# A new instruction order, and other engines for some copies, in a fused attention and gated feed-forward kernel

## The chip, the cores and the metric

The kernel runs on one NeuronCore of a Trainium2 chip. The metric is the device time of one execution in microseconds (us). Of the kernel before there are three timed runs.

## What is computed

Eight batches of eight heads, 576 tokens, head size 64. A small set of 32 packed queries p attends to k and v; then q attends to the packed result, which is key and value at once. The output, as 4608 tokens of 512, goes through a feed-forward network with d_ff = 2048.

```python
def sm_attn(qq, kk, vv):
    s = scale * np.matmul(qq, kk.transpose(0, 1, 3, 2))
    s = s - np.max(s, axis=-1, keepdims=True)
    a = np.exp(s)
    a = a / (np.sum(a, axis=-1, keepdims=True) + 1e-09)
    return np.matmul(a, vv)
p_packed = sm_attn(p, k, v)
out = sm_attn(q, p_packed, p_packed)
...
h = x @ w_in
g = h * (1.0 / (1.0 + np.exp(-1.702 * h)))
return (g @ w_out).astype(np.float32)
```

## The kernel before, in words

**Precision.** Everything is float32. An operand of the large matrix products is held in two parts, an upper part (a cast to fp32r) and a lower part (the rest), and a product is three matmuls: upper by upper, upper by lower, lower by upper. The upper part is made by a plain copy that may run on either of two engines (`move`: L111 is the copy on ScalarE, L113 the one on another engine, here VectorE). The lower part is a subtraction on VectorE.

**Attention.** For each batch b, `scores1_mm` (L275) makes the scores of the packed queries in two halves of 288 keys, `scores1_copy` takes them out of PSUM, `scores1_max` and `bias1` find the maximum, `exp1` (L331) exponentiates with a sum, the result is transposed through DRAM (or on TensorE for batches 0 and 1), `pack` (L415) multiplies by v. `pack_turn_mm` turns the packed result into PT. `m_mm` (L454) multiplies PT by one of four column blocks c of w_in; `m_upper` and `m_lower` (L478) split it. `scores2_mm` (L498) makes the second scores, `scores2_turn`, `max2`, `sub2`, `exp2` (L535), `sum2`, `norm2`, `turn2` the second softmax; `a_upper` and `a_lower` (L572) split it. So x itself is never made: h = a times m.

**Feed-forward.** d_ff is cut into two halves (phases). In a phase, for each batch, half of its tokens and each block u of 256 columns, `h_mm` (L604) makes h with two groups of six matmuls in a pair of PSUM banks. `g_main` (L621) takes 256 tokens, `g_over` (L626) the 32 that are left over, both on ScalarE with the gelu table; the left-over tokens of four batches are gathered into one more block, "over". `g_over` is the last reader of the pair, and so frees it. Then come `g_sum` (L664, block sums on VectorE), `g_upper` (the cast of 128x896), `g_lower` (L682), and `prod` (L745): seven block products in place of eight, into the four accumulator banks A to D. Their weights are prepared the same way: `begin_w` (L198, ScalarE) and `join_w` (L226, VectorE) put the two halves of a word of the raw load together, `wa_upper` and `wa_lower` (L236) split it, `w_diff` (L259) makes the block differences T, `wb_upper` and `wb_lower` split those. Batch 0 is done with plain products (`prod0`, L703). `c_take` copies a full accumulator to SBUF. Phase 0 stores these partial results to DRAM; phase 1 loads them, adds (`c_sum`), combines the blocks (`c_comb`) and stores the output.

**What sets the order.** The program runs under a manual schedule: each engine's instructions are issued as the steps stand in one tuple, `order` (from L812), 2878 steps long. The loop at its end runs them. A step may end with the engine that does its copy (`dve` or `act`); without one it is the function's default. The attention of batch b+1 is interleaved with the products of batch b all through phase 0. `warm` (L119) puts matmuls of the identity where TensorE would stand idle at the start.

**Buffers that make engines wait.** PSUM has one pool with two pairs of banks, shared by h, both scores, the packing and m; and four accumulator banks. In SBUF there are three buffers each for X, gs, a and m, two for r, and two for raw weights. exp and gelu are in different tables of ScalarE, so each change loads a table.

**Tiled and full.** A matmul of `scores1_mm`, `pack`, `m_mm` and `scores2_mm` uses a tile of 64x32 (or 128x32) of the TensorE array, the others the whole array. One matmul of float32 is two records in a trace; the order below counts it once.

Of the kernel before, what the change touches and what calls it, by code (L numbers as in the profile page):

```python
# [21 lines left out]
def kernel(  # L22
# [787 lines left out]
    dve, act, pool = nc.vector, nc.scalar, nc.gpsimd  # L810
    table(AF.Exp)
    order = (  # L812
        (load, "k", 0, 0), (load, "k", 0, 1), (load_w, "in", 0, 0, 0), (load_w, "in", 0, 1, 0),
# [10 lines left out]
        (load_w, "in", 0, 0, 1), (pack_end, 0), (load_q0, 1), (warm, 4, 2, "D"), (pack_turn_mm, 0),
        (pack_turn_copy, 0), (warm, 5, 1, "D"), (scores2_mm, 0, 0), (begin_w, "in", 0, 3, 0),
        (join_w, "in", 0, 3, 0), (load_w, "out", 0, 0, None), (begin_w, "in", 0, 1, 1),
        (scores2_turn, 0, 0, 0), (m_mm, 0, 0, 0), (join_w, "in", 0, 1, 1), (begin_w, "in", 0, 2, 1),
        (max2, 0, 0, 0), (m_upper, 0, 0, 0), (join_w, "in", 0, 2, 1), (load_w, "out", 1, 0, None),
        (scores2_turn, 0, 0, 1), (sub2, 0, 0, 0, pool), (begin_w, "in", 0, 3, 1), (warm, 6, 3, "B"),
        (m_lower_mm, 0, 0, 0), (begin_w, "in", 0, 0, 1), (max2, 0, 0, 1), (exp2, 0, 0, 0),  # L830
        (join_w, "in", 0, 3, 1), (m_lower_copy, 0, 0, 0), (load_w, "out", 2, 0, None),
        (sum2, 0, 0, 0), (sub2, 0, 0, 1, pool), (exp2, 0, 0, 1), (join_w, "in", 0, 0, 1),
        (sum2, 0, 0, 1), (norm2, 0, 0, 0, pool), (load_w, "out", 3, 0, None), (turn2, 0, 0, 0),
        (warm, 7, 6, "B"), (scores2_mm, 0, 1), (m_mm, 0, 0, 1), (m_upper, 0, 0, 1),
        (norm2, 0, 0, 1, pool), (scores2_turn, 0, 1, 1), (a_upper, 0, 0, 0, 0), (load, "k", 1, 0),
        (scores2_turn, 0, 1, 0), (warm, 8, 3, "D"), (m_lower_mm, 0, 0, 1),
        (begin_w, "out", 0, 0, None), (turn2, 0, 0, 1), (a_lower_mm, 0, 0, 0, 0), (max2, 0, 1),
        (begin_w, "out", 1, 0, None), (a_upper, 0, 0, 0, 1), (join_w, "out", 0, 0, None),
        (t_store, 0, 0), (a_lower_copy, 0, 0, 0, 0), (warm, 9, 4, "D"), (a_lower_mm, 0, 0, 0, 1),
        (m_lower_copy, 0, 0, 1), (join_w, "out", 1, 0, None), (load, "v", 1, 0),  # L840
        (begin_w, "out", 2, 0, None), (sub2, 0, 1), (a_lower_copy, 0, 0, 0, 1),
        (join_w, "out", 2, 0, None), (exp2, 0, 1), (warm, 10, 5, "D"), (h_mm, 0, 0, 0, 0, 0),
        (wa_upper, 0, 0, 4, dve), (begin_w, "out", 3, 0, None), (h_mm, 0, 0, 0, 0, 1), (sum2, 0, 1),
        (wa_lower_mm, 0, 0), (load_w, "in", 1, 0, None), (g_main, 0, 0, 0, 0),
        (join_w, "out", 3, 0, None), (wa_lower_mm, 0, 1), (norm2, 0, 1), (load_w, "in", 1, 1, None),
        (wa_lower_copy, 0, 1), (turn2, 0, 1), (g0_upper, 0, 0, 0), (t_store, 0, 1),
        (wa_lower_copy, 0, 0), (g0_lower, 0, 0, 0), (a_upper, 0, 0, 1), (load, "k", 1, 1),
        (warm, 11, 11, "D"), (prod0, 0, 0, 0, 0), (wa_upper, 1), (a_lower, 0, 0, 1),
        (g_over, 0, 0, 0, 0), (wa_lower, 1), (begin_w, "in", 1, 0, None), (h_mm, 0, 0, 1, 0, 0),
        (load, "v", 1, 1), (h_mm, 0, 0, 1, 0, 1), (join_w, "in", 1, 0, None),  # L850
        (begin_w, "in", 1, 1, None), (h_mm, 0, 0, 0, 1, 0), (load_w, "in", 1, 2, None),
        (g_main, 0, 0, 1, 0), (join_w, "in", 1, 1, None), (h_mm, 0, 0, 0, 1, 1),
        (g_over, 0, 0, 1, 0), (g0_upper, 0, 1, 0), (load_w, "in", 1, 3, None),
        (h_mm, 0, 0, 1, 1, 0), (g0_lower, 0, 1, 0), (g_main, 0, 0, 0, 1), (h_mm, 0, 0, 1, 1, 1),
        (g0_upper, 0, 0, 1), (g_over, 0, 0, 0, 1), (g0_lower, 0, 0, 1), (prod0, 0, 1, 0, 1),
        (g_main, 0, 0, 1, 1), (g_over, 0, 0, 1, 1), (begin_w, "in", 1, 2, None),
        (prod0, 0, 1, 0, 0), (join_w, "in", 1, 2, None), (begin_w, "in", 1, 3, None),
        (load_w, "out", 4, 0, None), (prod0, 0, 0, 1, 0), (g0_upper, 0, 1, 1),
        (join_w, "in", 1, 3, None), (g0_lower, 0, 1, 1), (load_w, "out", 5, 0, None), (m_mm, 0, 1),
        (scores1_mm, 1, 0), (m_upper, 0, 1), (prod0, 0, 1, 1, 1), (scores1_copy, 1, 0, 0, dve),  # L860
        (scores1_copy, 1, 0, 1), (m_lower, 0, 1), (begin_w, "out", 4, 0, None), (scores1_mm, 1, 1),
        (join_w, "out", 4, 0, None), (h_mm, 0, 0, 0, 2, 0), (scores1_copy, 1, 1, 0),
        (load, "q", 1, 0), (begin_w, "out", 5, 0, None), (scores1_max, 1, 0), (h_mm, 0, 0, 0, 2, 1),
        (load_w, "out", 6, 0, None), (scores1_copy, 1, 1, 1), (join_w, "out", 5, 0, None),
        (h_mm, 0, 0, 1, 2, 0), (g_main, 0, 0, 0, 2), (bias1, 1, 0), (scores1_max, 1, 1),
        (exp1, 1, 0), (load_w, "out", 7, 0, None), (prod0, 0, 1, 1, 0), (wa_upper, 2, 0, 4, dve),
        (bias1, 1, 1), (wa_lower, 2), (load, "q", 1, 1), (prod0, 0, 0, 0, 1), (exp1, 1, 1),
        (sum1, 1, 0), (g_over, 0, 0, 0, 2), (sum1, 1, 1), (h_mm, 0, 0, 1, 2, 1),
        (g0_upper, 0, 0, 2, dve), (g0_lower, 0, 0, 2), (prod0, 0, 0, 1, 1),
        (begin_w, "out", 6, 0, None), (g_main, 0, 0, 1, 2), (join_w, "out", 6, 0, None),  # L870
        (h_mm, 0, 0, 0, 3, 0), (g_over, 0, 0, 1, 2), (begin_w, "out", 7, 0, None),
# [779 lines left out]
```

## Time and profile before

| what | value |
| --- | --- |
| timed runs | 696.09, 697.15, 698.79 us; median 697.15 us |
| the profiled execution's own time | 696.48 us |
| its span, first to last instruction | 694.7 us |
| TensorE matmul busy | 670.9 us |
| TensorE weight load busy (beside matmuls) | 606.6 us |
| VectorE busy | 564.5 us |
| ScalarE busy | 378.4 us |
| GpSimd busy | 4.6 us |
| mean granted TensorE clock | 0.994 |
| DMA | 105.04 MB, mean 151 GB/s |

Busy times of the engines overlap. The chain of work that ended last is 79% TensorE, 8% ScalarE, 6% VectorE and 3% DMA. The span is shorter than the execution's own time by 1.8 us, which lie around it. Phase 0 with its attention fills the span up to about 357 us; from there to about 400 us the left-over tokens of phase 0 and the weights of phase 1 cross; phase 1 follows, and the last 11 us are additions and stores.

[...] `a<-b` reads: b is read, a is written; a pool or engine in `[...<-...]` ended the gap before that instruction.

### The profile page before, as it was taken

The numbers are of one execution on the slowest core, as the hardware profiler recorded it, in microseconds if no ns is written. First come the engines' busy times: TensorE is split into PE (matmuls) and PEld (weight loads), VectorE is DVE, ScalarE is ACT, GpSimd is POOL, SyncE is SP. The second block draws the span as 40 slices with busy tenths as digits, with TensorE's granted clock in tenths as the row PEclk, the third lists the DMA queues.
The fourth block names the chain that finished last, engine by engine and source line by source line (L and its number), as shares of the span: only waits on it lengthen the run. The fifth ranks groups of instructions, "written<-read, shape, count | busy, mean of one in ns | idle before, by whom it ended". The sixth has DMA issues, their size and how long they took to land.

```text
span 694.7 us, 15288 instructions
## 1 busy us (share of the span) xinstructions
PE 670.9 (97%) x6256; PEld 606.6 (87%) x6256; DVE 564.5 (81%) x1161; ACT 378.4 (54%) x694; POOL 4.6 (1%) x14
## 2 busy tenths in 40 slices
PE   8999899999999999999999899999999999999993
PEld 6878698888989899888999689899998999799993
DVE  2869989968798997987989745889889888786894
ACT  4878676758566484775947643433243344443430
POOL 1100000000000000000000000000000000000000
PEclk9999999999999999999999999999999999999997
DMA  9965645746556456471674513323432232223321
...
DMA packets 58901, 105.04 MB, mean 151 GB/s; under 512 B 31312, under 2 KB 35792, under 8 KB 57808
## 3 DMA queue, kind: packets, MB, share of 16 engines
...
q14 instruction: 20, 0.16, 0.1%
...
## 4 chain that ended last, share of the span: by engine, by line
PE 79%; ACT 8%; DVE 6%; DMA 3%; issue 2%; DVEq 0%; POOL 0%; ACTq 0%; POOLq 0%
PE h L604 25%; PE accA L745 10%; PE accC L745 10%; PE accB L745 10%; PE accD L745 5%; PE psm_None L454 4%; DMA raw_in_None<-w_in 2%; PE ps L498 2%; DMA raw_out_None<-w_out 1%; PE accB_over L745 1%; PE pspv L415 1%; PE accD L703 1%; PE accB L703 1%; PE accC L703 1%; PE accA_over L745 1%
## 5 line engine op out<-in xcount | busy, mean ns | idle before, releaser
L604 PE MATMUL h<-a,m 128*128 128x288 f32 x1536 | 228.1, 297 | 7.1 <-ACT over L626 5.2
L604 PEld LDWEIGHTS h<-a,m 128*128 128x128 f32 x1536 | 209.6, 188 | 17.6 <-ACT over L626 8.1
L682 DVE TENSOR_TENSOR gs<-X,gs 128x896 fp32r<-128x896 f32 x112 | 120.5, 1086 | 22.7 <-ACT gs L111 21.4
L621 ACT ACTIVATE X<-h 128x512 f32<-128x512 f32 x128 | 75.4, 599 | 110.2 <-PE h L604 91.4
L111 ACT CAST gs<-X 128x896 fp32r<-128x896 f32 (+1 forms) x100 | 88.7, 895 | 67.5 <-DVE X L664 25.8
L664 DVE TENSOR_TENSOR X<-X 128x256 f32<-128x256 f32 (+1 forms) x336 | 103.2, 329 | 22.7 <-ACT X L621 20.3
L745 PE MATMUL accC<-Wa,gs 128*128 128x256 f32 x672 | 99.0, 284 | 0.2 <-ACT r L111 0.2
L745 PE MATMUL accB<-Wb,gs 128*128 128x256 f32 x672 | 98.7, 283 | 0.0
L745 PEld LDWEIGHTS accB<-Wb,gs 128*128 128x128 f32 x672 | 87.7, 188 | 6.8 <-issue 6.8
L745 PEld LDWEIGHTS accC<-Wa,gs 128*128 128x128 f32 x672 | 87.9, 189 | 4.8 <-issue 4.3
L745 PE MATMUL accD<-Wa,gs 128*128 128x256 f32 x336 | 59.6, 286 | 0.4 <-ACT r L111 0.3
L745 PE MATMUL accA<-Wa,gs 128*128 128x256 f32 x336 | 59.0, 284 | 0.0
L745 PE MATMUL accA<-Wb,gs 128*128 128x256 f32 x336 | 58.1, 282 | 0.0
L745 PEld LDWEIGHTS accD<-Wa,gs 128*128 128x128 f32 x336 | 48.0, 188 | 6.3 <-issue 3.5
L745 PEld LDWEIGHTS accA<-Wa,gs 128*128 128x128 f32 x336 | 48.2, 189 | 1.7 <-DVE X L664 0.8
L745 PEld LDWEIGHTS accA<-Wb,gs 128*128 128x128 f32 x336 | 47.8, 189 | 0.0
L111 ACT CAST m<-psm_None 128x1024 fp32r<-128x1024 f32 x29 | 29.2, 1015 | 27.9 <-PE psm_None L454 24.4
L478 DVE TENSOR_TENSOR m<-psm_None,m 128x1024 fp32r<-128x1024 f32 x31 | 37.6, 1218 | 5.9 <-ACT m L111 5.5
L454 PE MATMUL psm_None<-w_in,PT 64*32 64x512 f32 x496 | 33.7, 598 | 0.2 <-DVE x L508 0.2
L572 DVE TENSOR_TENSOR a<-xt,a 128x576 fp32r<-128x576 f32 x31 | 23.0, 745 | 8.2 <-ACT a L111 8.0
L626 ACT ACTIVATE over<-h 128x64 f32<-128x64 f32 x128 | 27.3, 226 | 0.0
L621 ACT ACT_TABLE_LOAD x16 | 20.5, 1283 | 3.9 <-PE h L604 3.7
...
## 6 DMA issues: line engine op xcount, KB each, us to landing
...
```

The source lines that it names most:

```text
L111: nc.scalar.copy(dst, src)
L454: nc.tensor.matmul(banks[eo][32 * j : 32 * j + 32], PT[rows(eo), j, :], w_in_sb[c % 2][rows(eo), j, at], start=True, stop=True,)
L478: nc.vector.tensor_tensor(m[:, 1, :, at], st["bank", "m", b, c, part], m[:, 0, :, at].bitcast(F32), op=ALU.subtract,)
L498: nc.tensor.matmul(bank[32 * j : 32 * j + 32, eo, :NH], st["PT", b][rows(eo), j, :], kq["q0", half][rows(eo), j, :] if b == 0 else kq["q", ...
L572: engine.tensor_tensor(even_odd(a[:, 1], eo), even_odd(st["t", 2, b, half], eo), even_odd(a[:, 0], eo).bitcast(F32), op=ALU.subtract,)
L604: nc.tensor.matmul(h, m[:, part, eo, at], a[:, ap, eo * NH : (eo + 1) * NH], start=(n == 0), stop=(n == len(terms) - 1),)
L621: nc.scalar.activation(X[:, :4].rearrange("p (f t) n -> p f (t n)", f=2), h[:, :, :NM], AF.Gelu_apprx_sigmoid, scale=2.0)
L626: nc.scalar.activation(over_part(ph, b, half, u), st["h", ph, b, half, u][:, :, NM:NH], AF.Gelu_apprx_sigmoid, scale=2.0,)
L664: engine.tensor_tensor(to, a, b_, op=ALU.subtract)
L682: engine.tensor_tensor(lo, X, hi.bitcast(F32), op=ALU.subtract)
L703: nc.tensor.matmul(accs[name], gs[:, gp, 2 * f + r], W[:, wp, 2 * f : 2 * f + 2].rearrange("p n e -> p (n e)"), start=(u == 0 and f == 0 a ...
L745: nc.tensor.matmul(acc[:, n * HC : (n + 1) * HC], gs[:, gp, g], Wa[:, wp, w] if w < 4 else Wb[:, wp, w - 4], start=(u == 0 and n == 0 and ...
```

## The change

The functions are the same. The tuple `order` is replaced by another, of 2879 steps, which holds the same computation in a different sequence, with different engines for some copies and other counts of warm matmuls (58 before, 54 now). TensorE's program has 966 rows before and 963 after. Instructions of VectorE go from 1161 to 1129, those of ScalarE from 641 to 673 in the program (table loads not counted); GpSimd's 12 and SP's 231 stay as many. Moved from VectorE to ScalarE are 26 `g_upper`, 10 `c_take`, 8 `a_upper`, 7 `scores1_copy`, 3 `wb_upper`, 2 `m_upper` and a few more; the other way go 8 `g_upper`, 6 `c_take`, 5 `scores1_copy`, 3 `wb_upper`, 2 `g0_upper` and the `wa_upper` of blocks 6 and 7. The diff replaces some 800 lines of the tuple; these are its pieces at scores1 of batch 6 and at the crossing between the phases.

```diff
-        (scores1_mm, 6, 0), (g_over, 0, 5, 0, 1), (prod, 0, 4, 1, 2, "A"), (g_sum, 0, 5, 0, 0, 2),
-        (a_upper, 0, 5, 1), (t_store, 5, 1), (g_sum, 0, 5, 0, 1, 1), (g_sum, 0, 5, 0, 0, 3),
-        (scores1_mm, 6, 1), (scores1_copy, 6, 0, 0), (g_sum, 0, 5, 0, 1, 2), (a_lower, 0, 5, 1),
+        (g_over, 0, 5, 0, 1), (scores1_mm, 6, 0), (g_sum, 0, 5, 0, 1, 1), (a_upper, 0, 5, 1),
+        (g_sum, 0, 5, 0, 0, 2), (scores1_mm, 6, 1), (g_sum, 0, 5, 0, 1, 2), (t_store, 5, 1),
...
-        (c_take, "over", 1, "C"), (h_mm, 1, 0, 0, 0, 1), (c_take, "over", 1, "B"), (wb_lower, 4, 0),
-        (h_mm, 1, 0, 1, 0, 0), (c_store, "over", 1), (w_diff, 5, 3), (h_mm, 1, 0, 1, 0, 1),
-        (w_diff, 5, 2), (join_w, "out", 14, 0, None), (wb_upper, 5, 0), (w_diff, 5, 4),
-        (load_w, "in", 3, 1, None), (begin_w, "in", 3, 0, None), (w_diff, 6, 2), (wb_lower, 5, 0),
-        (wa_upper, 7), (c0_load, 0), (join_w, "in", 3, 0, None), (w_diff, 6, 4),
+        (c_take, "over", 1, "C"), (w_diff, 6, 3), (w_diff, 6, 2), (h_mm, 1, 0, 0, 0, 0),
+        (w_diff, 5, 2), (c_take, "over", 1, "B"), (w_diff, 6, 4), (wb_upper, 6, 0),
+        (h_mm, 1, 0, 0, 0, 1), (c_store, "over", 1), (wb_lower, 4, 0), (wb_upper, 5, 0),
+        (h_mm, 1, 0, 1, 0, 0), (wb_lower, 6, 0), (begin_w, "in", 3, 2, None), (h_mm, 1, 0, 1, 0, 1),
+        (w_diff, 5, 4), (wb_lower, 5, 0), (c0_load, 0), (wa_upper, 6, 0, 4, dve),
+        (wa_upper, 7, 0, 4, dve), (join_w, "in", 3, 1, None), (w_diff, 7, 1), (g_main, 1, 0, 0, 0),
```

The order of TensorE around scores1 of batch 6, before (a row is a line of the kernel, the operation, what it writes and reads, the size and how often; the numbers in a name are phase, batch, half and block, and last a running number; scores1 is `ps1_`):

```order
L745 MATMUL accD_0_4_1_3285<-Wa_2_660,gs_0_4_1_2_3326 128x256 x3
L275 MATMUL ps1_6_0_3369<-k_6_3099 32x288 x8
L745 MATMUL accA_0_4_1_3214<-Wa_2_660,gs_0_4_1_2_3326 128x256 x3
L745 MATMUL accA_0_4_1_3214<-Wb_2_882,gs_0_4_1_2_3326 128x256 x3
L275 MATMUL ps1_6_1_3392<-k_6_3099 32x288 x8
L745 MATMUL accB_0_4_1_3313<-Wb_2_882,gs_0_4_1_2_3326 128x256 x6
L604 MATMUL h_0_5_0_2_3417<-a_0_5_0_3238,m_5_1_3283 128x288 x12
```

and now:

```order
L745 MATMUL accB_0_4_1_3178<-Wb_2_874,gs_0_4_1_2_3315 128x256 x6
L745 MATMUL accD_0_4_1_3360<-Wa_0_418,gs_0_4_1_0_3095 128x256 x3
L275 MATMUL ps1_6_0_3369<-k_6_3109 32x288 x8
L275 MATMUL ps1_6_1_3382<-k_6_3109 32x288 x8
L745 MATMUL accD_0_4_1_3360<-Wa_1_467,gs_0_4_1_1_3167 128x256 x3
L604 MATMUL h_0_5_0_2_3405<-a_0_5_0_3241,m_5_1_3287 128x288 x6
L745 MATMUL accD_0_4_1_3360<-Wa_2_656,gs_0_4_1_2_3315 128x256 x3
L604 MATMUL h_0_5_0_3_3420<-a_0_5_0_3241,m_5_1_3287 128x288 x12
```

The two halves of scores1 (L275) stand together, where two products stood between them.

The order of TensorE at the crossing, before, from the last product of phase 0's left-over tokens:

```order
L745 MATMUL accB_0_over_1_4986<-Wb_3_1219,gs_0_over_1_3_5015 128x256 x6
L604 MATMUL h_1_0_0_0_5007<-a_1_0_0_4649,m_0_2_4923 128x288 x6
L604 MATMUL h_1_0_1_0_5122<-a_1_0_1_4652,m_0_2_4923 128x288 x12
L604 MATMUL h_1_0_0_1_5165<-a_1_0_0_4649,m_0_2_4923 128x288 x12
L703 MATMUL accB_1_0_0_5185<-Wa_4_5017,gs_1_0_0_0_5163 128x512 x6
```

and now:

```order
L745 MATMUL accB_0_over_1_5003<-Wb_3_1020,gs_0_over_1_3_5024 128x256 x6
L604 MATMUL h_1_0_0_0_5111<-a_1_0_0_4647,m_0_2_4715 128x288 x12
L604 MATMUL h_1_0_1_0_5134<-a_1_0_1_4658,m_0_2_4715 128x288 x12
L604 MATMUL h_1_0_0_1_5167<-a_1_0_0_4647,m_0_2_4715 128x288 x12
L604 MATMUL h_1_0_1_1_5183<-a_1_0_1_4658,m_0_2_4715 128x288 x12
L703 MATMUL accA_1_0_0_5204<-Wa_4_5011,gs_1_0_0_0_5165 128x512 x6
```

The first h of phase 1 (`h_1_0_0_0`) had one of its two groups earlier, among the over products; now both, and all of `h_1_0_1_0`, stand behind them, and the first `prod0` comes after one h more.

The order of ScalarE at the same place, before, from the copy of the last over accumulator:

```order
L111 COPY r_0_over_1_5070<-accB_0_over_1_4986 128x512
L111 CAST Wb_5_5140<-T_5_5082 128x768
L198 CAST top0_80<-raw_in_3_0_None_5062 128x512
L111 CAST Wa_7_5148<-E_6_7_4893 128x1024
L621 ACTIVATE X_1_0_0_0_5159<-h_1_0_0_0_5007 128x512
L626 ACTIVATE over_1_0_0_5161<-h_1_0_0_0_5007 128x2x32
```

and now:

```order
L111 COPY r_0_over_1_5067<-accB_0_over_1_5003 128x512
L111 CAST Wb_6_5121<-T_6_5100 128x768
L111 CAST Wb_5_5132<-T_5_5088 128x768
L198 CAST top0_80<-raw_in_3_2_None_5059 128x512
L621 ACTIVATE X_1_0_0_0_5161<-h_1_0_0_0_5111 128x512
L626 ACTIVATE over_1_0_0_5163<-h_1_0_0_0_5111 128x2x32
```

Ahead of the first `g_main` of phase 1 (L621) a `Wa` cast is gone and a `Wb` cast stands in its place; the `Wa` casts of blocks 6 and 7 are on VectorE.

## Rows read from the trace of the kernel before

**Rows 1.** The page's busy time, share of the span and instructions of each engine.

```profile
PE 670.9 (97%) x6256; PEld 606.6 (87%) x6256; DVE 564.5 (81%) x1161; ACT 378.4 (54%) x694; POOL 4.6 (1%) x14
```

**Rows 2.** Busy us by stretch: PE, PEld, DVE, ACT, POOL; clock, DMA share, GB/s.

```profile
43.00:357.00 314.00, 307.03 (x3233) 270.52 (x3227) 270.75 (x556) 211.55 (x377) 0.00 (x0) 1.00 0.56 180
357.00:400.00 43.00, 39.80 (x310) 34.40 (x316) 37.00 (x71) 29.00 (x50) 0.00 (x0) 1.00 0.57 201
400.00:660.00 260.00, 260.00 (x2138) 245.90 (x2127) 208.49 (x425) 102.34 (x193) 0.00 (x0) 1.00 0.30 92
```

**Rows 3.** TensorE's timeline in the second half: start, length, line, operation, operands, count.

```profile
590.64 0.86 PE L745 MATMUL accB<-Wb,gs 128*128 128x256 f32 x6
591.34 0.88 PE L745 MATMUL accC<-Wa,gs 128*128 128x256 f32 x6
...
593.21 1.95 PE L454 MATMUL psm_None<-w_in,PT 64*32 64x512 f32 x32
595.09 0.62 PE L745 MATMUL accD<-Wa,gs 128*128 128x256 f32 x3
...
602.03 1.09 PE L454 MATMUL psm_None<-w_in,PT 64*32 64x512 f32 x16
...
604.98 0.97 PE L745 MATMUL accB<-Wb,gs 128*128 128x256 f32 x6
605.79 0.88 PE L745 MATMUL accC<-Wa,gs 128*128 128x256 f32 x6
```

**Rows 4.** TensorE's timeline at the crossing of the halves [gap before <-what ended it].

```profile
379.45 2.54 PE L604 MATMUL h<-a,m 128*128 128x288 f32 x18
384.61 1.92 PE L604 MATMUL h<-a,m 128*128 128x288 f32 x12 [2.62 <-ACT over L626]
```

**Rows 5.** ScalarE's timeline at the same place.

```profile
379.68 0.59 ACT L111 COPY r_over<-accB_over 128x512 f32<-128x512 f32 x1
381.54 0.83 ACT L111 CAST Wb<-T 128x768 fp32r<-128x768 f32 x1 [1.28 <-DVE T L259]
382.28 0.76 ACT L198 CAST top<-raw_in_None 128x512 f16<-128x512 bf16 x1
382.91 1.03 ACT L111 CAST Wa<-E 128x1024 fp32r<-128x1024 f32 x1
383.85 0.59 ACT L621 ACTIVATE X<-h 128x512 f32<-128x512 f32 x1
384.34 0.21 ACT L626 ACTIVATE over<-h 128x64 f32<-128x64 f32 x1
```

**Rows 6.** TensorE's timeline, products of the remainder tokens ahead of the crossing.

```profile
367.88 0.59 PE L745 MATMUL accA_over<-Wa,gs_over 128*128 128x256 f32 x3 [0.58 <-DVE r L113]
```

**Rows 7.** TensorE's timeline behind an exp2 of batch 7.

```profile
336.21 1.87 PE L604 MATMUL h<-a,m 128*128 128x288 f32 x12 [0.17 <-ACT over L626]
```

**Rows 8.** TensorE's timeline at the exp1 of batch 7.

```profile
299.19 0.52 PE L745 MATMUL accD<-Wa,gs 128*128 128x256 f32 x3
...
303.45 2.67 PE L604 MATMUL h<-a,m 128*128 128x288 f32 x18 [1.59 <-ACT over L626]
```

**Rows 9.** TensorE's timeline at scores1 of batches 3 and 5.

```profile
122.72 0.72 PE L275 MATMUL ps<-k 64*32 64x288 f32 x16 [0.22 <-ACT over L626]
...
209.19 0.72 PE L275 MATMUL ps<-k 64*32 64x288 f32 x16 [0.48 <-issue]
```

**Rows 10.** Groups of instructions: busy us, mean ns | gaps before, what ended them.

```profile
L604 PE MATMUL h<-a,m 128*128 128x288 f32 x1536 | 228.1, 297 | 7.1 <-ACT over L626 5.2 <-DVE m L478 1.2 <-ACT x L111 0.4
```

**Rows 11.** TensorE's timeline, an accumulator that waits for its copy, batch 2.

```profile
151.17 0.98 PE L745 MATMUL accC<-Wa,gs 128*128 128x256 f32 x6 [0.18 <-ACT r L111]
```

**Rows 12.** TensorE's timeline, warm matmuls ahead of the first products.

```profile
29.25 2.62 PE L119 MATMUL accD_warm<-ident 128*128 128x128 f32 x22
```

**Rows 13.** Groups of instructions: the gs cast on ScalarE and on VectorE.

```profile
L111 ACT CAST gs<-X 128x896 fp32r<-128x896 f32 x85 | 79.4, 943 | 67.4 <-DVE X L664 25.8 <-PE accC L745 16.5 <-issue 4.8
...
L113 DVE CAST gs<-X 128x896 fp32r<-128x896 f32 x27 | 16.8, 621 | 5.8 <-PE accC L745 4.7 <-PE accB L745 0.7
```

More of the change, by code (lines that the diff above doesn't have):

```diff
@@ L824 @@
[L824 to L871, printed above, removed]
@@ new lines @@
+        (scores2_turn, 2, 1, 1), (scores2_turn, 2, 1, 0), (load, "v", 3, 0),
+        (prod, 0, 1, 1, 3, "B"), (a_lower, 0, 2, 0), (m_upper, 2, 0), (max2, 2, 1), (m_mm, 2, 1),
+        (c_take, 1, 1, "B"), (m_lower, 2, 0), (prod, 0, 1, 1, 1, "C"), (load, "v", 3, 1),
+        (m_upper, 2, 1), (sub2, 2, 1), (h_mm, 0, 2, 0, 0, 0), (m_lower, 2, 1), (exp2, 2, 1),
+        (h_mm, 0, 2, 0, 0, 1), (prod, 0, 1, 1, 2, "C"), (sum2, 2, 1), (g_main, 0, 2, 0, 0),
+        (h_mm, 0, 2, 0, 1, 0), (norm2, 2, 1), (h_mm, 0, 2, 0, 1, 1), (g_sum, 0, 2, 0, 0, 1),
@@ new lines @@
+        (prod, 0, 2, 1, 3, "C"), (a_lower, 0, 3, 0), (m_upper, 3, 0), (max2, 3, 1), (m_mm, 3, 1),
+        (load, "v", 4, 1), (m_lower, 3, 0), (prod, 0, 2, 1, 3, "A"), (t_store, 3, 0),
+        (m_upper, 3, 1), (sub2, 3, 1), (h_mm, 0, 3, 0, 0, 0), (c_take, 2, 1, "A"), (m_lower, 3, 1),
+        (exp2, 3, 1), (h_mm, 0, 3, 0, 0, 1), (c_take, 2, 1, "C"), (prod, 0, 2, 1, 3, "D"),
+        (sum2, 3, 1), (g_main, 0, 3, 0, 0), (h_mm, 0, 3, 0, 1, 0), (h_mm, 0, 3, 0, 1, 1),
+        (c_take, 2, 1, "D", dve), (norm2, 3, 1), (prod, 0, 2, 1, 3, "B"), (g_over, 0, 3, 0, 0),
@@ new lines @@
+        (m_mm, 6, 1), (g_upper, 0, 5, 1, 3), (load, "v", 7, 1), (m_lower, 6, 0),
+        (prod, 0, 5, 1, 1, "D"), (m_upper, 6, 1), (prod, 0, 5, 1, 2, "B"), (sub2, 6, 1),
+        (prod, 0, 5, 1, 2, "D"), (g_lower, 0, 5, 1, 3), (exp2, 6, 1), (h_mm, 0, 6, 0, 0, 0),
+        (h_mm, 0, 6, 0, 0, 1), (m_lower, 6, 1), (prod, 0, 5, 1, 3, "A"), (g_main, 0, 6, 0, 0),
+        (sum2, 6, 1), (h_mm, 0, 6, 0, 1, 0), (h_mm, 0, 6, 0, 1, 1), (norm2, 6, 1),
+        (c_take, 5, 1, "A"), (prod, 0, 5, 1, 3, "C"), (g_sum, 0, 6, 0, 0, 1), (g_over, 0, 6, 0, 0),
@@ new lines @@
+        (prod, 1, 4, 0, 0, "D"), (m_upper, 5, 2), (m_lower, 4, 3), (prod, 1, "over", 0, 3, "B"),
+        (prod, 1, 4, 0, 1, "D"), (c_sum, "over", 0, "B"), (prod, 1, 4, 0, 0, "A"), (m_lower, 5, 2),
+        (h_mm, 1, 4, 0, 2, 0), (h_mm, 1, 4, 0, 2, 1), (c_comb, "over", 0, 1),
+        (prod, 1, 4, 0, 1, "A"), (c_comb, "over", 0, 2), (g_main, 1, 4, 0, 2),
+        (c_comb, "over", 0, 3), (h_mm, 1, 4, 0, 3, 0), (g_sum, 1, 4, 0, 2, 1), (g_over, 1, 4, 0, 2),
+        (store, "over", 0, 0), (c_comb, "over", 0, 5), (h_mm, 1, 4, 0, 3, 1),
@@ L1609 @@
+        (c_comb, "over", 1, 1), (c_comb, "over", 1, 4), (c_comb, "over", 1, 3),
+        (c_comb, "over", 1, 5), (c_comb, "over", 1, 2), (c_sum, "over", 1, "C"),
+        (store, "over", 1, 0), (store, "over", 1, 1, act),
     )
```

1486 lines of the change are left out of this document (750 added, 736 removed).

## The prediction

> **What bounds the kernel now.** I read the busy shares first, then the same busy times stage by stage, then the timeline of TensorE around each place where it waits. TensorE is busy 97% of the span, VectorE 81%, ScalarE 54% [rows 1]. By stages: the second half of d_ff (400 to 660 us) is TensorE without a gap, 260.00 of 260 us. In the first half, with the attention between the products (43 to 357 us), TensorE is busy 307.03 of 314 us, so 6.97 us of gaps, with VectorE at 270.75 and ScalarE at 211.55. At the crossing between the halves (357 to 400 us) it is idle for 3.20 us [rows 2]. [...]
>
> **Tiled runs.** Only the order and some engines change. The order of TensorE's instructions has 57 runs of tiled matmuls (L275, L415, L454, L498) between full ones before, and 50 after: the two halves of scores1 of batches 3 to 7 that stood apart are brought together, and m_mm pairs in the second half. In the trace, start to start [rows 3]: two runs of 16 records with a group of six between them and one behind take 605.79 - 602.03 = 3.76 us. Merged, it is one run of 32 (595.09 - 593.21 = 1.88), the group behind it (605.79 - 604.98 = 0.81) and a group that touches no tiled run (591.34 - 590.64 = 0.70): 3.39. That is 0.37 per merged run. The same sum over scores1, where shorter groups lie between, gave me 0.35, and I take that: 7 x 0.35 = **-2.45 us**. If only the tail of a tiled run is saved (1.02 x 2 - 1.88 = 0.16), it is -1.1; the other end is 7 x 0.37 = -2.6. Nothing else covers this, it is TensorE's own time; but behind a late VectorE it would turn into a wait (a rival below).
>
> **The crossing.** Before, the h group at 384.61 waits 2.62 us for a pair bank that g_over frees; three groups of six stood between the last over product and it, 2.54 us in all, so some 0.8 each [rows 4]. ScalarE was late because it had no work for 1.28 us until a T block came from VectorE, and then did a Wb cast, a top cast and a Wa cast ahead of g_main [rows 5]. After, the Wa casts of blocks 6 and 7 are VectorE's, the T blocks are made earlier, and four h groups instead of three stand ahead of the blocked one. ScalarE from the accB_over copy to g_over's end is then 0.5 + 0.74 + 0.74 + 0.63 + 0.49 + 0.2 = 3.3 us, by the spacings in [rows 5]; TensorE covers 4 x 0.8 = 3.2 of it; the copy may start a little after those groups do, for it waits for the last product's end. I leave 0.2 to 0.4 of the wait: **-2.4 us** (from -2.7, no wait, to 0, should T be late again; late next would be VectorE's two added Wa casts). The wait of 0.58 us at 367.88, for a VectorE copy of accA [rows 6], goes: the copy is on ScalarE and some 2.9 us of products stand between. With the slower first group behind it that is **-0.75**. Two h groups that wait behind exp2's table load (0.17 us of gap and slower matmuls behind it; [rows 7] has the first) get g_over ahead of that load: -0.35 each, **-0.7** together (0 to -0.7).
>
> **Exp windows.** After scores1 of a batch, ScalarE copies scores, loads a table, does two exps, loads the table back and only then frees an h bank. In batch 7 this costs 1.59 us [rows 8]: four product groups (2.7 us) stood in front of that h, now eight (42 matmuls, 5.0 us), while ScalarE gets one gs cast (0.85 start to start) more in between; its 4.26 us from 299.19 to 303.45 become 5.1, so 0.1 to 0.2 is left. With the slower first group that gain is 1.55. But by the same count of batches 2, 3 and 6, where casts are added to ScalarE and no cover, waits grow by 0.85, 0.5 and 0.35, and in 4 and 5 they shrink by 0.3. Sum **-0.2** (from -1.5 to +1.5). The halves of scores1 that waited for a bank [rows 9] are placed later in batches 3 and 5 (-0.8 and -0.55, the gap and the slow matmuls on both sides of it), but in batch 4 the second half now stands right behind the first, with 6.7 us of ScalarE work in the new order against 5.5 us of TensorE's, both by the spacings in this trace: +1.3. Sum **-0.05**. Where h follows m_lower more closely (batches 3 and 4) I add 0.4 each, **+0.8**; such waits cost 1.2 us in the whole trace before [rows 10]. The accumulators of batch 2 that waited for c_take copies behind an exp2 table [rows 11] are half relieved: **-0.5** (0 to -1).
>
> **Start.** The first 43 us hang on raw weight loads through two buffers; TensorE is filled up there with warm matmuls. There are four fewer of them, at 2.62 / 11 = 0.24 us each [rows 12], so at most -0.95. The join of w_out and the first g cast go to a freer engine: **-0.6** (0 to -0.95). DMA issues are moved, none is added; they land well ahead of use outside this stretch, so I cost them at nothing. One that is late there would be seen as a longer gap before the first products. The end of the kernel (c_comb and stores) is unchanged.
>
> **Moved copies.** Net 32 copies go from VectorE to ScalarE, above all gs casts (27 on VectorE become 7). Such a cast takes 943 ns on ScalarE and 621 on VectorE [rows 13]. I cost the extra time at nothing, because ScalarE is idle for 102 us of the 314 in the first half [rows 2] and those casts had 67.4 us of idle before them [rows 13]; the VectorE chain sum, cast, lower gets room. If that cover is gone, the third rival comes.
>
> **Sum.** -2.45 - 2.4 - 0.75 - 0.7 - 0.2 - 0.05 + 0.8 - 0.5 - 0.6 = -6.85 us. A new order of the first half also makes small waits I cannot see in a trace that doesn't have it. I allow a third of the 6.97 us of gaps which the present order has there, +2.3 (0 to 5). Net -4.55. From the profiled execution's 696.48 that gives 691.93; the median of the runs lies 0.67 above that execution, so **692.6 us**.
>
> **Rivals.**
> 1. *No new waits*: what I see closes and nothing opens, 692.6 - 2.3 = 690.3. For: the places are spread out, and most had cover. Against: the 20 gs casts alone bring ScalarE 20 x 0.94 = 19 us, nearly all in the first half. 0.15.
> 2. *Savings become waits*: in the first half VectorE sets the pace (86% busy, and every product needs sum, cast and lower first), so merging and better cover there only make TensorE wait for gs; only the three merges of the second half and the crossing count: -1.05 - 2.4 - 0.75 + 2.5 = -1.7, 695.4. For: VectorE's load. Against: of TensorE's waits before h, 5.2 us of 7.1 end with ScalarE, and 1.2 with VectorE [rows 10]. 0.25.
> 3. *ScalarE late at the banks (slower)*: the moved casts stand ahead of g_main and g_over in the fifteen stretches of exp1 and exp2 in the first half, each delaying a bank by one cast of 0.85 us: +12.75 - 6.85 = +5.9, 703. It decides from where ScalarE's idle time ahead of the release is shorter than the cast; batch 7 had 1.59 us of that kind already. Against: the idle time in [rows 13]. 0.10.
> [...]
> That the change does not do what it says I leave out: the order shows the runs merged.
>
> **Numbers.** A measurement of this kernel tells about 0.5% from no change, so faster is below 693.66 and slower above 700.6. My forecast has 0.50; four fifths of it lie below 693.66, and rival 1 wholly, rival 2 by a tenth: 0.41 + 0.15 + 0.02 = 0.58. Slower is most of rival 3, 0.08. Same is the rest, 0.34. The range takes rivals 1 and 2 with the bounds of the terms (crossing, exp windows, allowance): 688.5 to 698; rival 3 and the far ends stay out.
>
> **What would show it.** Right: 50 tiled runs, the merged scores1 groups of 32 records in batches 3 to 7; the wait at the crossing under 0.5 us; none at the change of batch 7 above 0.3; TensorE's idle in the first half at 5 to 7 us; a new wait of about 1 us before the second half of scores1 of batch 4. Wrong: idle of TensorE in the first half over 9 us, ended by ScalarE's g_over or casts (rival 3) or by VectorE's lowers (rival 2); or a second half that is shorter by more than 1.5 us, which would say I undersized a change between tiled and full.

## The result and the profile after

The changed kernel takes 687.0 us in the median of four runs (685.64 to 687.95), the kernel before 697.09 us (four runs). The ratio is 0.9851, 95% interval 0.9826 to 0.9877. So it is faster by 10.1 us, in the direction that was forecast and by more than twice the forecast 4.5 us, and the time lies below the range. The traces are of one execution each, with a span of 683.8 us where it was 694.7; the one of the changed kernel is its fastest run, so differences between the two traces come out some 0.7 us larger than between the medians.

The page's busy times, and then the same by stretch with the columns of [rows 2] (PE is TensorE, PEld its weight loads, DVE VectorE, ACT ScalarE, POOL GpSimd; a granted clock of 1.00 is full speed):

```profile
PE 664.8 (97%) x6248; PEld 604.9 (88%) x6248; DVE 554.7 (81%) x1129; ACT 403.1 (59%) x726; POOL 4.5 (1%) x14
```

```profile
43.00:357.00 314.00, 309.93 (x3286) 275.55 (x3283) 269.88 (x552) 228.97 (x402) 0.00 (x0) 1.00 0.59 189
357.00:400.00 43.00, 42.11 (x315) 36.75 (x315) 36.05 (x64) 27.73 (x52) 0.00 (x0) 1.00 0.42 134
```

TensorE's idle time in the first half falls from 6.97 to 4.07 us (314 - 309.93), at the crossing from 3.20 to 0.89. In the first half ScalarE is busier by 17 us, and VectorE hardly less. The groups of instructions that answer to [rows 10, 13]:

```profile
L604 PE MATMUL h<-a,m 128*128 128x288 f32 x1536 | 223.5, 296 | 3.0 <-DVE m L478 1.2 <-ACT over L626 1.2 <-ACT x L111 0.3
...
L111 ACT CAST gs<-X 128x896 fp32r<-128x896 f32 x105 | 98.2, 945 | 76.8 <-DVE X L664 19.3 <-PE accC L745 18.4 <-issue 8.3
...
L113 DVE CAST gs<-X 128x896 fp32r<-128x896 f32 x7 | 4.4, 625 | 0.7 <-PE accA L745 0.5
```

Of TensorE's 5.2 us ahead of h that ended with g_over, 1.2 are left. The 105 gs casts now on ScalarE take the same 0.94 us each as the 85 did, and have 76.8 us of idle time ahead of them in all, where it was 67.4 (0.73 us for each, where it was 0.79).

Where the time went can be told by places in the work that both programs have:

| stretch of work | before, us | after, us | difference | forecast |
| --- | --- | --- | --- | --- |
| start to the first block product (L745) | 86.48 | 86.44 | 0.0 | -0.6 |
| from there to the last block product of the first half | 293.13 | 285.40 | -7.7 | -1.3 |
| from there to the last matmul | 303.70 | 300.94 | -2.8 | -2.7 |
| additions and stores behind it | 11.38 | 11.07 | -0.3 | 0 |

(The forecasts are sums of the prediction's terms; the six h matmuls, 0.8 us, that now stand behind the last product of the first half are counted in the second and third row.) The miss is all in the second row.

Another cut adds up, over all matmul records, by how much each starts later than the usual spacing behind the one before it. Waits with the matmul that waited: 15.7 us before, 8.8 after, -6.9. Tiled runs and the matmuls next to them: -2.4. Matmuls away from both: -1.3, of which -1.0 are slow matmuls right behind a wait, fewer because the waits are fewer (twelve of h took 1.92 us behind the wait of 2.62 [rows 4], and 1.75 without a wait, at 300.50 below). Four warm matmuls less give -0.9, and the first 43 us without them +1.0. Together -10.5, and the end gives -0.3.

TensorE at the crossing, which answers to [rows 4], and ScalarE there, which answers to [rows 5]:

```profile
370.97 0.87 PE L745 MATMUL accB_over<-Wb,gs_over 128*128 128x256 f32 x6
371.68 3.33 PE L604 MATMUL h<-a,m 128*128 128x288 f32 x24
375.74 3.42 PE L604 MATMUL h<-a,m 128*128 128x288 f32 x24 [0.72 <-ACT over L626]
```

```profile
372.39 0.58 ACT L111 COPY r_over<-accB_over 128x512 f32<-128x512 f32 x1
372.86 1.57 ACT L111 CAST Wb<-T 128x768 fp32r<-128x768 f32 x2
374.33 0.78 ACT L198 CAST top<-raw_in_None 128x512 f16<-128x512 bf16 x1
...
375.46 0.22 ACT L626 ACTIVATE over<-h 128x64 f32<-128x64 f32 x1
```

The chain from the accB_over copy to g_over's end is 375.68 - 372.39 = 3.29 us, as summed in the prediction, and four h groups stand in front. The copy began 0.55 us after the last product, behind that of accC; 0.72 us of the wait of 2.62 is left.

TensorE at batch 7's exp1, which answers to [rows 8]: the last of eight product groups, and h behind them without a gap:

```profile
300.14 0.53 PE L745 MATMUL accA<-Wb,gs 128*128 128x256 f32 x3
300.50 1.75 PE L604 MATMUL h<-a,m 128*128 128x288 f32 x12
```

And scores1 of batch 4 with both halves together, the new wait that was forecast (the two gaps and the slow matmuls around them come to 1.1 us):

```profile
162.39 0.72 PE L275 MATMUL ps<-k 64*32 64x288 f32 x16 [0.16 <-ACT over L626]
163.28 4.22 PE L604 MATMUL h<-a,m 128*128 128x288 f32 x30 [0.18 <-DVE x L113]
```

### The profile page after: what moved, and what is told of

Its sections match the earlier page's. It is cut to its first block, busy times and chain, and to the rows that moved or that the text cites. A ratio compares the mean times of both kernels' runs of the same rounds, so it can differ in the third digit from the quotient of the medians.

```text
span 683.8 us, 15288 instructions
## 1 busy us (share of the span) xinstructions
PE 664.8 (97%) x6248; PEld 604.9 (88%) x6248; DVE 554.7 (81%) x1129; ACT 403.1 (59%) x726; POOL 4.5 (1%) x14
## 4 chain that ended last, share of the span: by engine, by line
PE 83%; ACT 6%; DMA 5%; DVE 4%; issue 1%; SPq 0%; DVEq 0%; ACTq 0%
PE h L604 27%; PE accA L745 11%; PE accC L745 11%; PE accB L745 11%; PE accD L745 6%; PE psm_None L454 4%; PE accD L703 2%; DMA q<-q 2%; PE accC L703 1%; PE accB L703 1%; PE ps L498 1%; DMA v<-v_last 1%; PE pspv L415 1%; PE accA L703 1%; PE accB_over L745 1%
## 5 line engine op out<-in xcount | busy, mean ns | idle before, releaser
L604 PE MATMUL h<-a,m 128*128 128x288 f32 x1536 | 223.5, 296 | 3.0 <-DVE m L478 1.2
L111 ACT CAST gs<-X 128x896 fp32r<-128x896 f32 (+1 forms) x119 | 106.8, 907 | 78.9 <-DVE X L664 19.3
L621 ACT ACTIVATE X<-h 128x512 f32<-128x512 f32 x128 | 75.6, 600 | 88.2 <-PE h L604 77.7
L745 PE MATMUL accC<-Wa,gs 128*128 128x256 f32 x672 | 99.1, 283 | 0.0
L745 PE MATMUL accB<-Wb,gs 128*128 128x256 f32 x672 | 98.3, 282 | 0.0
L745 PEld LDWEIGHTS accC<-Wa,gs 128*128 128x128 f32 x672 | 87.9, 189 | 5.2 <-issue 4.2
L745 PEld LDWEIGHTS accB<-Wb,gs 128*128 128x128 f32 x672 | 87.6, 189 | 3.8 <-issue 3.0
L745 PE MATMUL accA<-Wa,gs 128*128 128x256 f32 x336 | 59.5, 286 | 0.0
L745 PE MATMUL accD<-Wa,gs 128*128 128x256 f32 x336 | 59.4, 286 | 0.0
L745 PE MATMUL accA<-Wb,gs 128*128 128x256 f32 x336 | 58.0, 281 | 0.0
L745 PEld LDWEIGHTS accD<-Wa,gs 128*128 128x128 f32 x336 | 48.2, 188 | 5.6 <-issue 4.5
L745 PEld LDWEIGHTS accA<-Wa,gs 128*128 128x128 f32 x336 | 47.9, 189 | 3.4 <-issue 3.1
L745 PEld LDWEIGHTS accA<-Wb,gs 128*128 128x128 f32 x336 | 47.8, 189 | 0.0
L111 ACT CAST m<-psm_None 128x1024 fp32r<-128x1024 f32 x31 | 30.8, 1016 | 22.8 <-PE psm_None L454 19.5
```

The lines of the kernel that those rows point to most:

```text
L111: nc.scalar.copy(dst, src)
L604: nc.tensor.matmul(h, m[:, part, eo, at], a[:, ap, eo * NH : (eo + 1) * NH], start=(n == 0), stop=(n == len(terms) - 1),)
L621: nc.scalar.activation(X[:, :4].rearrange("p (f t) n -> p f (t n)", f=2), h[:, :, :NM], AF.Gelu_apprx_sigmoid, scale=2.0)
L745: nc.tensor.matmul(acc[:, n * HC : (n + 1) * HC], gs[:, gp, g], Wa[:, wp, w] if w < 4 else Wb[:, wp, w - 4], start=(u == 0 and n == 0 and ...
```

## The experiments

Three theories stood against each other. **A**: the order closed the waits, and it does not matter which engine makes a copy. **B**: the copies taken off VectorE closed them. **C**: a change between tiled and full matmuls costs far more than the 0.35 us I took.

### Order and engines apart

One kernel has the new order, with all 84 moved copies on their old engines; the second the same for the 34 gs casts alone; the third the old order with the new engines. Examples of each kind, as in the first:

```diff
-        (g_upper, 0, 1, 0, 0)
+        (g_upper, 0, 1, 0, 0, 0, 7, dve)
...
-        (c_take, 2, 0, "A", dve)
+        (c_take, 2, 0, "A")
...
-        (wb_upper, 1, 1, dve)
+        (wb_upper, 1, 1)
```

> The new order, with all 84 moved copies back on the engines they had before. The gain to explain is 697.1 - 687.0 = 10.1 us. Theory A (the order closed the waits, the engines are indifferent): 686.5 to 689, TensorE's gaps stay at 6 to 8 us. Theory B (VectorE's relief closed the waits): 691 to 695, with new gaps of TensorE in the first half that end with VectorE. Theory C (the price of changing between tiled and full is larger than I took it): 686.5 to 689, since the 50 tiled runs stay.

> The new order, with only the 34 moved gs casts back on their old engines. Theory A: 686.5 to 688.5. Theory B: at least half of what the first kernel of this call loses to VectorE, so 690 to 694 if that one is at 691 to 695. Theory C: 686.5 to 688.5.

> The old order, with the 84 copies on the engines of the new version. Theory A: 696 to 700, since the old order has no room in ScalarE's queue ahead of the banks. Theory B: 690 to 694, most of the gain without the order. Theory C: 696 to 698.

Measured: 705.13 us (703.97 to 707.37; ratio to the kernel before 1.0116, 1.0087 to 1.0145), 690.26 us (0.9897, 0.9872 to 0.9923) and 704.62 us (1.0109, 1.0082 to 1.0135). None of the theories said this: the first and the third kernel lie about 10 us above the upper ends of B's ranges, and above A's and C's too; only the second lies in a range, B's. The order alone makes the old kernel 1.2% slower, the engines alone 1.1% slower, and together they make it 1.5% faster. TensorE's first half, in the columns of [rows 2], with the new order and old engines, then with the new order and old gs engines, then with the old order and new engines:

```profile
43.00:357.00 314.00, 301.34 (x3188) 264.33 (x3187) 264.54 (x544) 209.04 (x371) 0.00 (x0) 0.99 0.54 176
```

```profile
43.00:357.00 314.00, 308.52 (x3260) 273.19 (x3261) 271.52 (x555) 218.55 (x390) 0.00 (x0) 1.00 0.57 186
```

```profile
43.00:357.00 314.00, 301.94 (x3177) 264.67 (x3162) 258.12 (x532) 218.63 (x386) 0.00 (x0) 1.00 0.54 177
```

The gaps are 12.66, 5.48 and 12.06 us where the changed kernel has 4.07. What ended them differs. TensorE's waits from 43 us to the end, by the engine that ended them:

| order | engines | with ScalarE, us | with VectorE, us |
| --- | --- | --- | --- |
| old | old | 7.4 | 2.4 |
| new | old | 8.2 | 9.8 |
| old | new | 12.0 | 4.0 |
| new | new | 3.2 | 1.7 |

With the new order and old engines it is the waits for VectorE that grow (the two largest rows: total, times, longest). VectorE itself stood 3.06 us in batch 1, with all of its queue, for a cast that this kernel has on ScalarE and the changed kernel on VectorE:

```profile
PE h L604 <- ACT over L626: 4.0, 5, 2.2
PE h L604 <- DVE m L478: 2.6, 4, 1.2
```

```profile
66.79 0.43 DVE L272 TENSOR_TENSOR Wa<-r,Wa 128x256 fp32r<-128x256 f32 x1 [3.06 <-ACT Wa L111]
```

With the old order and new engines it is above all ScalarE at the banks, 8.1 us ahead of h where the kernel before has 5.2 [rows 10]. That is the third rival's mechanism, but at three places (batch 3, batch 6 and the crossing) and not in fifteen; the other new waits are of 0.2 to 0.6 us each, for either engine. At the exp of batch 6 a gs cast stands between the two exps, and a gs cast and two copies between g_main and the g_over that frees the bank; h then waits 1.17 us, where it waited 0.19 before.

```profile
PE h L604 <- ACT over L626: 8.1, 7, 3.4
```

```profile
259.09 0.92 ACT L111 CAST gs<-X 128x896 fp32r<-128x896 f32 x1
...
262.51 0.60 ACT L621 ACTIVATE X<-h 128x512 f32<-128x512 f32 x1
263.00 0.93 ACT L111 CAST gs<-X 128x896 fp32r<-128x896 f32 x1
263.83 0.59 ACT L111 COPY r<-accA 128x512 f32<-128x512 f32 x1
264.31 0.38 ACT L111 COPY r<-accD 128x256 f32<-128x256 f32 x1
264.57 0.25 ACT L626 ACTIVATE over<-h 128x64 f32<-128x64 f32 x1
```

```profile
264.87 1.84 PE L604 MATMUL h<-a,m 128*128 128x288 f32 x12 [1.17 <-ACT over L626]
```

### The other moved copies

To see whether it is the load of VectorE or the place of each copy, the other two groups were put back one at a time (the edits are of the kinds shown above).

> The new order; of the moved copies only the 30 that read PSUM (16 c_take, 12 scores1_copy, 2 m_upper) are back on their old engines. Theory A2 (each place in the order is matched to its engine, so any group put back opens waits there): 689 to 693. Theory B2 (only the load of VectorE counts; net 8 copies come back to it, some 4 us of its 555): 687 to 688.5.

> The new order; of the moved copies only the other 20 (6 wb_upper, 3 wa_upper, 3 g0_upper, 8 a_upper) are back. Theory A2: most of what all 84 lost ahead of 100 us (7.1 us) and at the crossing (3.7 us) comes back here, 693 to 697, the loss before 100 us at least 4 us. Theory B2 (net 8 copies of a, 3.6 us of VectorE): 687 to 689.

Measured: 693.73 us (0.9964, 0.9951 to 0.9978) and 692.16 us (0.9925, 0.9902 to 0.9948). Both lie above theory B2's ranges, and the second a little below A2's. So it is the place, and not the load alone: with 8 and 6 copies net back on VectorE, 6.7 and 5.2 us are lost, most of it in the first half in the one and ahead of the first block product in the other (92.51 us in place of 86.44). Of those 6 us, 3 can be the execution's, for another one of the changed kernel reaches that point at 89.55 us (see the end). For the rest the trace shows the same stop of VectorE for 3.06 us as above, and TensorE's new waits behind it (0.74 and 1.60 us) end with VectorE; which of the 20 copies counts was not separated. At the crossing, where A2 looked for 3.7 us, the wait is 0.8 us longer than in the changed kernel. The row in the first case, an accumulator that waits for a c_take on VectorE:

```profile
262.33 0.59 PE L745 MATMUL accD<-Wa,gs 128*128 128x256 f32 x3 [1.34 <-DVE r L113]
```

The three groups one at a time lose 3.3, 6.7 and 5.2 us, all at once 18.1. The 3.3 us of the gs casts are the least sure: the intervals of the two ratios overlap by a little. All four are taken against 687.0 us; later runs of the changed kernel gave 684.91, so each is uncertain by some 2 us.

### The price of a tiled run

In the changed version, eight tiled pairs were set apart; in the old one, five were brought together; and in the second half of the changed one, nine m_mm were cut in two.

```diff
-        (scores1_mm, 6, 0), (g_sum, 0, 5, 0, 1, 1), (a_upper, 0, 5, 1),
-        (g_sum, 0, 5, 0, 0, 2), (scores1_mm, 6, 1), (g_sum, 0, 5, 0, 1, 2), (t_store, 5, 1),
+        (scores1_mm, 6, 0), (g_sum, 0, 5, 0, 1, 1), (a_upper, 0, 5, 1),
+        (g_sum, 0, 5, 0, 0, 2), (g_sum, 0, 5, 0, 1, 2), (t_store, 5, 1),
...
+        (prod, 0, 4, 1, 1, "D"), (scores1_mm, 6, 1),
```

> The new order and engines, with eight pairs of tiled groups that stand together set apart again by one other TensorE step (scores1 of batches 4, 5 and 6, m_mm of batch 4, and four m_mm in the second half): 58 tiled runs instead of 50. Theory A (0.35 us per run): +2.8, 689.8; less by the wait before scores1 of batch 4 (1.1 us), which should go, so 688.5 to 690. Theory C (most of the 10.1 us hangs on the seven runs, 1.2 us or more each): 694 to 698. Theory B: as A.

> The old version with five tiled pairs merged and nothing else (scores1 of batches 4, 5, 6, m_mm of batch 4, m_mm c = 2 and 3 of batch 2): 52 runs instead of 57. Theory A: 5 x -0.35 = -1.75 on TensorE, less a bank wait of up to 1 us at each of two or three scores1 pairs, so 695.5 to 698. Theory C: 690 to 692.

> The new version with nine m_mm of the second half split in the middle by one other TensorE step, in a stretch where TensorE has no gaps: 59 tiled runs instead of 50. Theory A (0.35 us per run): +3.2, 690.2, and no new gaps. If only the tail of a tiled run counts (0.16): +1.4, 688.4. Theory C (1.2 us or more per run): +10.8, 698.

Measured: 689.31 us (0.9882, 0.9859 to 0.9905), 702.97 us (1.0086, 1.0063 to 1.0109) and 696.15 us (0.9992, 0.998 to 1.0003). The first is theory A's price: by the sum over records, tiled runs and their neighbours take 3.3 us more for eight runs. In the second they take 2.35 us less for five. These sums also hold what differs at the start, where nothing was moved; place by place, start to start from the run to the fourteenth record behind it, a merge saves 0.26 to 0.38 us wherever nothing waits. Yet the second kernel is slower, by one merge. Two m_mm of batch 2 now need both pairs of banks at once, and one pair is held by an h of which one group is done and the other comes later. So the second m_mm waits until m_lower of the first has read its pair:

```profile
440.63 1.09 PE L454 MATMUL psm_None<-w_in,PT 64*32 64x512 f32 x16
445.44 1.09 PE L454 MATMUL psm_None<-w_in,PT 64*32 64x512 f32 x16 [3.72 <-DVE m L478]
```

Behind the wait TensorE runs at a granted clock of 0.57 for 4 us. In the row below that stretch has 18 weight loads, by which six take some 1.3 us; ahead of the wait, in the same trace, a product group of six took 437.61 - 436.90 = 0.71 us start to start. With the columns of [rows 2]:

```profile
446.00:450.00 4.00, 4.00 (x33) 3.54 (x18) 0.00 (x0) 0.00 (x0) 0.00 (x0) 0.57 0.02 4
```

Of the other four merges none makes a wait longer by over 0.3 us. So the mechanism of the first term stands by itself, but one merge that finds a bank taken costs more than all five save. The third experiment lies 6 us above theory A's 690.2 and near theory C's 698, but it does not measure what it was meant to. Cut in two, each half takes 0.97 us start to start, nearly what a whole m_mm takes in the trace before (603.05 - 602.03 = 1.02). By that reading the extra 1.0 us per cut is mostly matmul time:

```profile
555.91 1.04 PE L471 MATMUL psm_None<-w_in,PT 64*32 64x512 f32 x8
556.88 0.97 PE L759 MATMUL accC<-Wa,gs 128*128 128x256 f32 x6
557.78 1.06 PE L471 MATMUL psm_None<-w_in,PT 64*32 64x512 f32 x8
```

Theory C falls by the first, for which it had 694 to 698 us, and by the four merges of the second that open no wait.

### Waits that are left, and the start

Four places where TensorE still waits in the changed kernel were mended: m_mm of batch 1 with its split earlier, and three ScalarE steps moved behind the g_over that they stood ahead of. Then the three alone, twice, the second time beside the changed kernel. The three:

```diff
-        (scores1_mm, 4, 0), (c_take, 2, 1, "B"), (g_sum, 0, 3, 0, 1, 1), (g_over, 0, 3, 0, 1),
-        (t_store, 3, 1), (scores1_copy, 4, 0, 0),
+        (scores1_mm, 4, 0), (g_sum, 0, 3, 0, 1, 1), (g_over, 0, 3, 0, 1),
+        (t_store, 3, 1), (scores1_copy, 4, 0, 0), (c_take, 2, 1, "B"),
...
-        (wb_upper, 3, 1), (wb_upper, 3, 0, dve), (g_over, 0, 1, 0, 0), (g_main, 0, 1, 0, 1),
+        (wb_upper, 3, 0, dve), (g_over, 0, 1, 0, 0), (g_main, 0, 1, 0, 1),
...
+        (g_over, 0, 1, 0, 1), (wb_upper, 3, 1),
...
-        (begin_w, "in", 3, 2, None), (h_mm, 1, 0, 1, 0, 1),
+        (h_mm, 1, 0, 1, 0, 1),
...
+        (g_over, 1, 0, 0, 0), (begin_w, "in", 3, 2, None),
```

> The new version with four places mended where TensorE still waits: m_mm of batch 1 with its split moved ahead of six product groups (wait 1.25 us at 77.29), a c_take moved behind the g_over that frees the bank for scores1 of batch 4 (0.16 and 0.18), a wb_upper behind the g_over ahead of scores1 of batch 2 (0.66), a begin_w behind the g_over at the crossing (0.72). If each such wait is what stands ahead of the release on that engine: -1.1, -0.5, -0.3 and -0.6, together -2.5, 684.5. If other work ends later all the same (the softmax chain of batch 1, VectorE's weights at the crossing): 686 to 688.

> As the kernel with four places mended, but only the three small moves behind a g_over, not the m_mm of batch 1. By the first reading -1.4, 685.6; by the second 686.5 to 688.

> The changed version itself, unaltered, on the same chip as the next run, to compare the two directly: 685.5 to 688.

> The three moves behind a g_over again, beside the changed version. By the traces so far (the crossing's wait 0.72 to 0.24, scores1 of batch 2 0.66 to 0.36, batch 4 hardly changed) 0.7 to 1.5 us less than the changed version; if the gain of the first comparison was chance, the same within 0.5 us.

Measured: 689.39, 685.44, then 684.91 for the changed kernel itself and 685.82 beside it. With m_mm early the h of batch 1 waits 2.21 us for its cast of a, where it had waited 1.25 us for m_lower: the m_lower steps stand ahead of the softmax chain on VectorE now. The wait at the crossing is 0.72 and 0.34 us in two traces of the changed kernel, and 0.24 and 0.65 us in two with the three moves. So it differs as much between executions as between the kernels, and side by side there is no gain that can be measured.

Last, the start. Two profiles of the same changed kernel reach the first block product at 86.44 and at 89.55 us. In both, ScalarE stands ahead of the first exps with a cast that waits for a DMA. That cast and its join were moved behind the exps, alone and with the three moves:

```diff
-        (begin_w, "in", 0, 2, 0), (bias1, 0, 0), (join_w, "in", 0, 0, 0), (exp1_first, 0, 0),
-        (load_q0, 0), (join_w, "in", 0, 2, 0), (exp1_first, 0, 1), (bias1, 0, 1), (sum1, 0, 0),
+        (bias1, 0, 0), (join_w, "in", 0, 0, 0), (exp1_first, 0, 0),
+        (load_q0, 0), (exp1_first, 0, 1), (bias1, 0, 1), (sum1, 0, 0),
...
+        (exp1_first, 1, 1), (begin_w, "in", 0, 2, 0), (sum1, 0, 1), (join_w, "in", 0, 2, 0),
```

> The changed version with one thing mended at the start: the cast of the second raw w_in block, which waits for a DMA until 9.57 us in one profile and 10.84 in another, and its join, behind the four exps of batch 0 instead of ahead of them. If that wait is why the start gained nothing (predicted -0.6, measured 0) and why it lies 3 us apart between two executions of one kernel: the exps start at 8.5 to 9.5 us, the first block product at 85 to 86 us, 684 to 686 in all, with less spread. If the weights are late in any case (the chain of raw loads ends the start): no change, 685 to 687.5.

> The same with the three small moves behind a g_over as well. If both count: 683 to 685; if neither does: 685 to 687.5.

Measured: 685.57 us (0.9848, 0.9827 to 0.9869) and 686.59 us (0.9849, 0.9828 to 0.987). No gain. ScalarE in the changed kernel, and with the cast moved:

```profile
7.46 0.48 ACT L198 CAST top<-home 128x256 f16<-128x256 bf16 x1 [5.02 <-DMA home<-w_in]
9.57 0.48 ACT L198 CAST top<-home 128x256 f16<-128x256 bf16 x1 [1.63 <-DMA home<-w_in]
9.92 0.49 ACT L324 ACTIVATE x<-ps,nb 128x288 f32<-128x288 f32 x1
```

```profile
8.44 0.48 ACT L198 CAST top<-home 128x256 f16<-128x256 bf16 x1 [6.00 <-DMA home<-w_in]
9.03 0.50 ACT L324 ACTIVATE x<-ps,nb 128x288 f32<-128x288 f32 x1
...
14.52 0.48 ACT L198 CAST top<-home 128x256 f16<-128x256 bf16 x1 [1.78 <-DMA home<-w_in]
```

The exps start 0.9 us earlier, and the first block product still comes at 87.11 us: a later cast waits for its raw block instead. When the raw loads deliver differs between executions (the first cast at 7.46, 8.44 and, in the second profile of the changed kernel, 8.66 us). That is 1.2 of the 3.1 us between the two profiles of the changed kernel. Most of the rest goes with the granted clock, here from 10 to 20 us in the first and in the second, with the columns of [rows 2]:

```profile
10.00:20.00 10.00, 9.21 (x157) 7.01 (x157) 5.35 (x17) 8.13 (x26) 1.38 (x2) 1.00 1.03 405
```

```profile
10.00:20.00 10.00, 8.35 (x140) 6.20 (x139) 2.86 (x11) 6.10 (x19) 0.00 (x0) 0.83 1.03 395
```

The second profile is 1.2 us behind at ScalarE's cast at 14.66 us and 2.85 us behind at the first m_mm (19.28 in place of 16.43); in between, the matmuls of `pack` take 2.22 us in place of 1.32. TensorE had waited 1.51 us at 11.82 us, and 1.14 us at the same place in the first. The trace of the new order with all copies on their old engines shows 0.83 in this stretch too, with TensorE busy for 8.67 of the 10 us. What ends the start otherwise was not separated. None of these versions beats the changed kernel clearly.

## Why the prediction was wrong

The direction held, and so did the terms that rest on a row of the old trace. The size was off by 5.6 us in the median, nearly all of it between 86 and 372 us.

- **Tiled runs, -2.45: right.** The sum over records gives -2.4. One thing in the prediction was wrong: among the scores1 pairs only those of batches 4, 5 and 6 were brought together; those of 3 and 7 stood together before. The other four runs are m_mm. The count of seven holds.
- **The crossing, -2.4: right, a little high.** The wait is 1.9 us shorter, by the chain that was summed, and 2.3 in the second trace of the changed kernel. The wait for accA of the left-over tokens shrank by 0.4 (0.75 forecast), since another of 0.17 us came ahead of it. The two waits behind exp2 in batch 7 went, as forecast.
- **Scores1, -0.05: signs right.** Batch 4 got a wait that costs 1.1 us with its slow matmuls (1.3 forecast), and those of batches 3 and 5, 1.1 and 0.6, went (0.8 and 0.55 forecast). The accumulators of batch 2 lost all of their 1.1 us, where half was forecast.
- **Exp windows, -0.2: failed, they gave -2.1.** Batch 7 went as forecast. Of the waits that I added for casts on ScalarE in batches 2, 3 and 6 (1.7 us), only 0.35 came, in batch 2, and the small ones that batches 3 and 6 had went. ScalarE in batch 6, before:

```profile
250.94 0.71 ACT L111 COPY x<-ps 128x288 f32<-128x288 f32 x2
252.41 0.70 ACT L111 COPY x<-ps 128x288 f32<-128x288 f32 x2 [0.75 <-PE ps L275]
253.93 1.28 ACT L331 ACT_TABLE_LOAD   x1 [0.82 <-DVE nb L315]
...
258.67 0.93 ACT L111 CAST gs<-X 128x896 fp32r<-128x896 f32 x1
259.49 0.23 ACT L626 ACTIVATE over<-h 128x64 f32<-128x64 f32 x1
```

and after:

```profile
247.38 1.31 ACT L111 COPY x<-ps 128x288 f32<-128x288 f32 x4
248.55 1.81 ACT L111 CAST gs<-X 128x896 fp32r<-128x896 f32 x2
250.38 1.28 ACT L331 ACT_TABLE_LOAD   x1
...
255.59 0.23 ACT L626 ACTIVATE over<-h 128x64 f32<-128x64 f32 x1
```

  Before, one gs cast stands in this chain, at 258.67 us; after, there are two, and one `g_main` more. The two casts, 1.81 us, lie where ScalarE had stood idle for 0.75 us (second half of scores1) and 0.82 (the bias). And the merged scores1 lets all four copies go at once. From the start of the first scores1 on TensorE to the bank it is 259.72 - 250.03 = 9.69 us before and 255.82 - 246.56 = 9.26 after, with that added work in it. I had added the casts to a chain as if it had no idle, and had not let the merging shorten it.
- **m_lower, +0.8: did not come.** Waits of h on m_lower are 1.2 us in both, at batch 1.
- **The allowance, +2.3: failed, and the largest.** It rested on the old order's 6.97 us of gaps. In the new one the gaps of that stretch fell to 4.07 us, and of those 1.25 and 0.66, the largest, stood in the old one too (1.25 and 0.83). Waits that the old trace does not have came as well, the largest 0.32 and 0.46 us one behind the other in batch 1, but far less than closed.
- **Start, -0.6: nothing**, as the last experiment shows; why is open in part.

So the steps that failed are the allowance of +2.3 us for new waits, where the gaps fell by 2.9 us, and the exp windows, -2.1 in place of -0.2; m_lower, scores1 and the accumulators of batch 2 add some 2 us to the miss. Behind them stands one entry, "I cost the extra time at nothing". What it charges ScalarE with did cost nothing. But I took the moved copies for a charge that idle time hides, with some room for VectorE as a bonus I did not price. The runs show that they are not a side entry: with the old engines the new order has 12.7 us of gaps in the first half, more than the old one's 7.0, and the allowance I made was for just such an order. With its own engines it has 4.1. What each single copy gives was not measured. The sum took each step's cover from the old trace, where the cover belongs to the old pairing of order and engines.

The rivals. The first (690.3) was the nearest, and the result went past it. The second, savings that turn into waits for VectorE, is what the new order does without its engines, 705.13 us, some 10 us above the rival's price. The third, ScalarE late at the banks, is the largest part of what the new engines do in the old order, 704.62 us. That this is close to the rival's 703 is chance: the rival added fifteen delays of a bank and took off what the new order saves, and this kernel has three such delays and no new order. Both mechanisms are real, and the change avoids each with its other half. A gs cast takes longer on ScalarE after the change too, 945 against 625 ns on VectorE, but to put the casts back costs 3.3 us. What a cast takes did not tell what it is worth here, where VectorE is the busier engine (554.7 us against 403.1).
